# Two-layer decode: last row's kept pairs put between whole pairs, second MLP run for five rows and then three

## Chip, cores, metric

One core of one Trainium2 chip runs one program. The metric is the device time of one launch in microseconds (us). Ratios are the mean time of one kernel's fast runs over that of the other kernel's fast runs of the same rounds, so they are not quite the ratio of the medians quoted beside them. Single executions of the kernel before scattered over 1175.6 to 1181.9 us, so a difference of less than about 2 us needs several rounds, or a comparison inside the traces.

## The reference, cut to what matters

Eight rows (B) of one token each pass twice through attention over a cache and an MLP:

```python
x = x + A(layernorm(x))        # Hq=16, Hkv=8, Sk=4096, Dh=256, D=448
x = x + B(layernorm(x))        # S=1: the shifted part of B is zero, so B is an MLP, 448 -> 1792 -> 448
x = x + A(layernorm(x))        # the same caches again
x = x + B(layernorm(x))

# A, for each row b and each of the 8 cache heads h ("pair" b,h):
#   scores = q @ K[b,h].T / 16 ; p = softmax(scores) ; o = p @ V[b,h]     K, V: 4096 x 256 bf16
# then all heads' o @ wo
```

One pair reads 2 MB of K and 2 MB of V. Almost all of the 472 MB are these.

## The kernel before

All data comes through a ring of five buffers of 1 MB, filled by one DMA queue in a fixed order of chunks. A buffer is refilled when TensorE has used it up. K is transposed on TensorE (`tk`), evicted by VectorE and ScalarE (`ktr`), multiplied with the query (`ps`); then softmax, P*V into `pvb`, and `finish`, which transposes the result into `oT`. For the first 4.5 heads of a row the transposed K stays in SBUF (`keep`), so in the second layer such a *kept pair* needs only V (2 MB, the half-kept one 3 MB), a *whole pair* needs 4 MB. The order of all 128 pairs is fixed when the program is built:

```python
A  = lambda b: [(0, b, h) for h in range(kept_heads, HKV)]     # layer 0, whole
Bk = lambda b: [(0, b, h) for h in range(kept_heads)]          # layer 0, whole, K is kept
C  = lambda b: [(1, b, h) for h in range(kept_heads)]          # layer 1, kept
Dn = lambda b: [(1, b, h) for h in range(kept_heads, HKV)]     # layer 1, whole
...
        for i in range(kept_heads):
            seq += C(b)[i:i + 1]                # kept pairs of row b ...
            if b + 1 < B:
                seq += Bk(b + 1)[i:i + 1]       # ... between whole ones of row b+1
    seq += Dn(B - 1)                            # row 7: five kept pairs in a row, then three whole
```

Row-wise work (layernorm, projections, MLP) is cut into steps. `pump()`, called after each piece of attention, takes one step:

```python
    def outputs(lo, n):                          # o @ wo for n rows: 4 steps of 32 matmuls
        for c in range(KC):
            ...
                for t in range(32):
                    last = e.matmul(room(w, C_Y + c * B + lo, n), wo[:, t, row0(c):row0(c) + w],
                                    copies(oT[:, t // 2, t % 2, lo:lo + n], n), ...)
            op("pe", f, ...)
            yield
    # output(b, h): the same for one pair, 16 matmuls.  mix(lo, n): layernorm and MLP of n rows, 112 matmuls.
    # The matmul counts of outputs and mix do not depend on n.

    def after(g):                                # called when pair g is finished
        layer, b, h = seq[g]
        if layer == 0 or b == B - 1:
            side.append(output(b, h))
        if last_of[layer, b] != g:
            return
        if layer == 0:
            jobs.extend([mix(b, 1), queries(b, 1)])
        elif b == B - 2:
            jobs.extend([outputs(0, B - 1), mix(0, B - 1)])      # rows 0 to 6 at once
        elif b == B - 1:
            jobs.append(mix(B - 1, 1))                           # row 7 at the very end
```

I call `outputs` with the following `mix` *the block* below.

## Time and profile before

| | before |
|---|---|
| median of 3 | 1177.4 us (1176.41 to 1179.94) |
| bytes through the queue | 471.97 MB |
| TensorE (PE) busy | 932 us, 79% |
| last packet of the stream | 1157.9 us (packet records) |
| last P*V | 1159.1 us |
| end | 1175.9 us |

From the page of the kernel before: the span, the busy times, the one data queue, and the shares of the chain that ended last.

```profile
span 1175.9 us, 42204 instructions
...
PE 932.0 (79%) x19067; PEld 811.0 (69%) x19067; DVE 487.6 (41%) x1803; ACT 312.3 (27%) x891; POOL 105.4 (9%) x281
...
q1 hardware_dynamic: 70496, 471.97, 98.0%
...
DMA 51%; PE 35%; DVE 8%; issue 4%; POOL 1%; ACT 0%; SPq 0%; POOLq 0%; ACTq 0%
```

The queue is nearly always full and the chain is half waits for DMA.

The end of the kernel before, in windows of 20 us. The columns are busy time and instruction count of PE (TensorE matmuls), PEld (TensorE weight loads), DVE (VectorE), ACT (ScalarE) and POOL (GpSimd), then the granted TensorE clock, the DMA share, and GB/s.

```profile
1060.00:1080.00 20.00, 17.35 (x361) 15.47 (x365) 11.15 (x49) 6.13 (x17) 1.92 (x5) 1.00 1.02 418
1080.00:1100.00 20.00, 16.97 (x437) 14.14 (x437) 8.38 (x41) 5.17 (x20) 2.87 (x8) 1.00 1.01 415
1100.00:1120.00 20.00, 16.56 (x415) 13.53 (x413) 5.37 (x24) 2.69 (x10) 1.68 (x5) 0.91 0.97 393
1120.00:1140.00 20.00, 16.45 (x308) 14.25 (x305) 9.77 (x44) 4.45 (x13) 2.08 (x5) 0.83 0.89 331
1140.00:1160.00 20.00, 18.30 (x413) 15.61 (x411) 8.45 (x29) 5.79 (x16) 1.54 (x4) 1.00 0.79 303
```

From 1110 on the stream falls from 418 to 331 GB/s: *the hole*. (The 303 of the last window also holds the end of the stream.) The kept pairs of row 7 and the block of seven rows lie there together.

Some TensorE instructions of the same stretch, from the timeline of the kernel before. In brackets stands the idle time before the instruction and what ended it; "issue" means that nothing in the profile was waited for.

```profile
1108.97 0.42 PE L623 MATMUL ps<-qT,keep 128*128 128x48 bf16 x10 [1.87 <-issue]
...
1121.48 0.89 PE L465 MATMUL mm<-oT,wo_sb 128*128 128x21 bf16 x29 [0.87 <-issue]
...
1130.02 0.76 PE L449 MATMUL mm<-oT,wo_sb 128*64 128x24 bf16 x16 [1.89 <-DVE oT L722]
...
1157.91 0.61 PE L697 MATMUL pvb<-ring,pT 128*2 128x256 bf16 x16 [0.36 <-DVE os L718]
...
1159.10 0.61 PE L697 MATMUL pvb<-ring,pT 128*2 128x256 bf16 x16
```

In these lines TensorE stops for 0.9 to 1.9 us three times, inside and around the block. The last two lines are the P*V of the last pair; the last of them begins 16.8 us before the end.

### The profile page before, as it was taken

Reading aid. Unit: us, or ns where it says so; the run is one execution under the profiler, and the core shown is the slowest. Engines: PE = TensorE matmul, PEld = TensorE weight load, DVE = VectorE, ACT = ScalarE, POOL = GpSimd, SP = SyncE. Lnnn points to the kernel's source line nnn. Section 1 sums busy time; section 2 is a strip of 40 time slices with the busy share of each in tenths; the row PEclk is TensorE's granted clock in tenths of the full one; section 3 lists DMA queues with packets and bytes.
Section 4 is the critical chain, followed back from the end, with each engine's and each line's share of the span. In section 5 each row is a group of like instructions: output and inputs, shape, how many; then the busy total and the mean of one; then the engine's idle time right before and its main releaser. Section 6 shows DMA issues by size and latency. Waiting matters only on the chain.

```text
span 1175.9 us, 42204 instructions
## 1 busy us (share of the span) xinstructions
PE 932.0 (79%) x19067; PEld 811.0 (69%) x19067; DVE 487.6 (41%) x1803; ACT 312.3 (27%) x891; POOL 105.4 (9%) x281
## 2 busy tenths in 40 slices
PE   2777898779877887778887887778887887878886
PEld 2666777668766776667776776667766776767675
DVE  2333543345333543345333543345333553345243
ACT  1223322222223222232222322223222222232121
POOL 0000001100100011000110001100110011000100
PEclk8979989999989999999989999999999999999987
DMA  9999999999999999999999999999999999999993
GB/s 359 391 415 419 419 396 417 418 420 412 417 416 420 411 418 410 420 420 404 420 404 420 415 412 416 420 409 412 419 417 420 416 405 417 412 420 414 407 335 133
DMA packets 70676, 474.66 MB, mean 404 GB/s; under 512 B 7248, under 2 KB 13280, under 8 KB 13792
## 3 DMA queue, kind: packets, MB, share of 16 engines
q1 hardware_dynamic: 70496, 471.97, 98.0%
q8 instruction: 149, 2.44, 0.8%
q14 instruction: 31, 0.25, 0.1%
HBM read 471.93 MB, written 0.01 MB: 401 GB/s over the span
## 4 chain that ended last, share of the span: by engine, by line
DMA 51%; PE 35%; DVE 8%; issue 4%; POOL 1%; ACT 0%; SPq 0%; POOLq 0%; ACTq 0%
DMA ring<-in_A_k_cache_dram 51%; PE tk L599 16%; PE ps L623 6%; PE pvb L697 5%; PE mm L449 3%; DVE ktr L606 2%; PE mm L409 2%; PE mm L513 1%; PE pvb L715 1%; DMA ring<-in_A_v_cache_dram 1%; DVE keep L606 1%; DVE oT L722 1%; DVE sm L347 1%; DVE os L718 0%; DVE sm L329 0%
## 5 line engine op out<-in xcount | busy, mean ns | idle before, releaser
L599 PE MATMUL tk<-ident,ring 128*128 128x128 f32 x2944 | 407.5, 291 | 134.0 <-DMA ring<-in_A_k_cache_dram 133.6
L599 PEld LDWEIGHTS tk<-ident,ring 128*128 128x128 f32 x2944 | 343.7, 149 | 177.5 <-DMA ring<-in_A_k_cache_dram 169.3
L606 DVE COPY ktr<-tk 128x512 f32<-128x512 f32 x224 | 153.8, 689 | 192.5 <-PE tk L599 192.4
L604 ACT COPY ktr<-tk 128x512 f32<-128x512 f32 x224 | 129.8, 586 | 323.1 <-PE tk L599 323.0
L697 PE MATMUL pvb<-ring,pT 128*2 128x256 bf16 x4096 | 160.5, 276 | 34.6 <-DMA ring<-in_A_v_cache_dram 22.7
L623 PE MATMUL ps<-qT,keep 128*128 128x48 bf16 x4608 | 159.9, 184 | 5.6 <-issue 4.6
L606 DVE COPY keep<-tk 128x512 f32<-128x512 f32 x144 | 99.5, 691 | 145.3 <-PE tk L599 144.6
L623 PEld LDWEIGHTS ps<-qT,keep 128*128 128x128 bf16 x4608 | 145.3, 97 | 17.6 <-issue 11.5
L604 ACT COPY keep<-tk 128x512 f32<-128x512 f32 x144 | 84.3, 586 | 251.7 <-PE tk L599 251.7
L679 ACT ACTIVATE pT<-ps,nb 128x32 bf16<-128x32 f32 x256 | 76.6, 299 | 268.9 <-DVE nb L675 221.7
L623 PE MATMUL ps<-qT,ktr 128*128 128x48 bf16 x3584 | 129.5, 184 | 17.8 <-DVE ktr L606 8.9
L623 PEld LDWEIGHTS ps<-qT,ktr 128*128 128x128 bf16 x3584 | 115.6, 97 | 29.0 <-DVE ktr L606 22.3
L673 POOL PARTITION_ALL_REDUCE gm<-pm x128 | 45.6, 356 | 796.8 <-DVE pm L670 796.8
L697 PEld LDWEIGHTS pvb<-ring,pT 128*2 128x2 bf16 x4096 | 75.8, 82 | 58.6 <-DMA ring<-in_A_v_cache_dram 27.2
L703 DVE COPY ob<-pvb 128x256 f32<-128x256 f32 x128 | 53.7, 420 | 46.2 <-PE pvb L697 45.6
L684 POOL PARTITION_ALL_REDUCE dn<-rs x128 | 51.2, 400 | 150.8 <-ACT pT L679 150.8
L449 PE MATMUL mm<-oT,wo_sb 128*128 128x24 bf16 (+1 forms) x1152 | 52.7, 187 | 9.5 <-DVE oT L722 4.7
L715 PE MATMUL pvb<-ident,ob 128*128 128x128 f32 x256 | 53.8, 293 | 7.8 <-DVE ob L703 7.5
L409 PE MATMUL mm<-lnT,wq_sb 128*128 128x24 bf16 x864 | 48.2, 184 | 12.9 <-DVE lnT L368 10.2
L670 DVE TENSOR_REDUCE pm<-ps 128x2 f32<-128x64 f32 x128 | 28.6, 224 | 69.1 <-PE ps L623 68.5
L449 PEld LDWEIGHTS mm<-oT,wo_sb 128*128 128x128 bf16 (+1 forms) x1152 | 42.3, 101 | 19.7 <-DVE oT L722 16.6
L409 PEld LDWEIGHTS mm<-lnT,wq_sb 128*128 128x128 bf16 x864 | 39.7, 98 | 22.3 <-DVE lnT L368 10.4
(70 smaller groups left out, 487.3 us busy)
## 6 DMA issues: line engine op xcount, KB each, us to landing
ring<-in_A_v_cache_dram SPq DMA_DIRECT2D x256, 1024.0 KB, 10.3
ring<-in_A_k_cache_dram SPq DMA_DIRECT2D x184, 1024.0 KB, 10.8
wo_sb<-in_A_wo_dram SPq DMA_DIRECT2D x1, 3584.0 KB, 25.6
wq_sb<-in_A_wq_dram SPq DMA_DIRECT2D x3, 1024.0 KB, 11.1
w_sb<-in_B_w_dram SPq DMA_DIRECT2D x1, 1568.0 KB, 20.1
w_sb<-in_B_w_dram SPq DMA_DIRECT2D x3, 448.0 KB, 12.7
wqf_sb<-in_A_wq_dram SPq DMA_DIRECT2D x2, 256.0 KB, 14.3
w3f_sb<-in_B_w_dram SPq DMA_DIRECT2D x2, 112.0 KB, 13.5
```

Source lines behind the costliest of these rows:

```text
L409: last = e.matmul(room(P, at + t * B, n), cols(kc, t), copies(rhs, n), start=(kc == 1), stop=(kc == 0), skip_group_check=True)
L449: last = e.matmul(room(w, C_P + c, 1), wo[:, t, row0(c):row0(c) + w], copies(oT[:, t // 2, t % 2, b:b + 1], 1), start=(t == 4 * h), stop=( ...
L599: last = e.transpose(bank[:, j * P:(j + 1) * P], src[:, 4 * (f % 4) + j, :].bitcast(f32), ident4[:, :])
L604: op("act", lambda e: e.copy(flat, bank[:, :]), reads=[r_bank], writes=[r_kt])
L606: op("dve", lambda e: e.tensor_copy(flat, bank[:, :]), reads=[r_bank], writes=[r_kt])
L623: last = e.matmul(pst[:, at:at + 2 * N_REP].rearrange("p (r j) -> p r j", j=2), kt(i, c), repeated(qT[:, b, c, 2 * h:2 * h + 2]), start=(c ...
L673: op("pool", lambda e: e.partition_all_reduce(gm[q][0][:, :], pm[q][0][:, :], P, ReduceOp.max), reads=[pm[q][1]], writes=[gm[q][1]])
L679: return e.activation(pT[q][0][:, :, :].rearrange("p i j -> p j i")[:, j, :], pst[:, C_S:C_S + 2 * NI].rearrange("p (i j) -> p j i", j=2)[ ...
L684: op("pool", lambda e: e.partition_all_reduce(dn[q][0][:, :], rs[q][0][:, :], P, ReduceOp.add), reads=[rs[q][1]], writes=[dn[q][1]])
L697: last = e.matmul(pvb[at:at + 2, 0:DH], pT[q][0][:, a * HALF + i, :], v[:, i, :], start=(a == 0 and i < 4), stop=(a == 1 and i >= HALF - 4 ...
L703: op("dve", lambda e: e.tensor_copy(ob[:, :], pvb[:, 0:DH]), reads=[r_pv], writes=[r_ob])
L715: last = e.transpose(pvb[:, DH + c * P:DH + (c + 1) * P], ob[:, c * P:(c + 1) * P], ident4[:, :])
```

## The change

The intent: put row 7's kept pairs between whole pairs, as in the other phases, and make a kept pair the last of all, so that no transposes, scores and softmax stand between the last byte and the end. The block moves ahead, to the end of row 4; rows 5, 6 and 7 then send an output by pair and share the last MLP.

```diff
+N_SPARE = 2
+N_ONCE = 5
...
     second = [p_ for b in range(B - 1) for p_ in Dn(b)]
+    second, spare = second[:-N_SPARE], second[-N_SPARE:]
...
+        whole = Bk(b + 1) if b + 1 < B else spare + Dn(b)[:-1]
+        light = C(b)
+        if b == B - 1:
+            light[-2:] = light[:-3:-1]
         for i in range(kept_heads):
-            seq += C(b)[i:i + 1]
-            if b + 1 < B:
-                seq += Bk(b + 1)[i:i + 1]
-    seq += Dn(B - 1)
+            if b == B - 1 and i == kept_heads - 1:
+                seq += Dn(b)[-1:]
+            seq += light[i:i + 1] + whole[i:i + 1]
...
-        if layer == 0 or b == B - 1:
+        if layer == 0 or b >= N_ONCE:
             side.append(output(b, h))
...
-        elif b == B - 2:
-            jobs.extend([outputs(0, B - 1), mix(0, B - 1)])
-        elif b == B - 1:
-            jobs.append(mix(B - 1, 1))
+        elif b == N_ONCE - 1:
+            jobs.extend([outputs(0, N_ONCE), mix(0, N_ONCE)])
+        elif g == len(seq) - 1:
+            jobs.append(mix(N_ONCE, B - N_ONCE))
```

## The prediction

> **What bounds the kernel now.** DMA. The page shows 471.97 MB through one queue, 98% of 16 engines' span, and the chain that ended last is 51% waits for K chunks. Undisturbed 20 us windows move 419 to 422 GB/s. The Trainium skill, "DMA: Bandwidth & Descriptors", section Bandwidth, gives 425 GB/s for a large load with 435 as the fabric ceiling; this trace's plateau agrees. The change leaves the bytes alone; only time in which the queue is not full can be won.
>
> **Where it is not full at the end** (windows view, before): 415 GB/s in 1080-1100, 393 in 1100-1120, 331 in 1120-1140, 303 in 1140-1160 (the stream ends at about 1156.3). Against 419 the stretch 1100-1156.3 misses about 3.05 MB, 7.3 us. Cause, by the timeline: five kept pairs run in a row (ten V chunks issued in a row), then four whole pairs meet the seven-row MLP. PE is busy 9.7, 9.2 and 9.8 us of 10 in 1110-1120, 1130-1140 and 1140-1150, at a granted clock of 0.83 to 0.85 in 1110-1140; it waits 1.9 us for oT behind the layernorm on VectorE, and two "issue" gaps cost 1.3 and 1.9 us. Ring buffers come free 3 to 5 us apart instead of the 2.5 us that a 1 MB chunk takes.
>
> **After the stream:** 1156.3 to 1175.9. The last whole pair has transposes until 1154.8, scores, maximum, exponentials until 1157.6; its P*V runs at 1157.9 and 1159.1, 1.6 and 2.8 us after the last byte. Then 16 us of serial finish, output, layernorm, MLP, store.
>
> **What the change does.**
> - Reorders: kept pairs of row 7 alternate with whole ones (2 and 4 MB), and the last pair is a kept one, needing no K. Its softmax is done before its V lands, so the last P*V should run within 0.3 us of the landing. Gain about 2.5 us.
> - The seven-row output and MLP become five-row ones (4x32 plus 112 matmuls, the same count); the instruction order puts outputs beside pair 6,6 and the MLP beside the next pairs.
> - Adds a 16-matmul output for each pair of rows 5 and 6: 16 x 0.72 us = 11.5 us of PE, 4 us of it in the last 110 us.
> - The end MLP has three rows instead of one: same matmul count and width (copies fill 24 columns), vector work a little wider: +0.1 to 0.4 us.
>
> **On the path.** I expect the queue at 405-415 GB/s in the last 100 us rather than 419: earlier stretches with a one-row MLP show 397 to 406, and PE will be near 90% busy. That gives back about 3 of the 7.3 us: gain 4.5. With the tail 2.5: 7 us. Predicted 1170.5 us, 80% range 1164 to 1176. Chances: faster by over 2% 0.02, within 2% 0.97, slower 0.01.
>
> **What would show it.** Span about 1169. Windows: no 20 us stretch before the stream's end under 385 GB/s; stream over at about 1151-1152; from the last byte to the end about 17 us, not 19.6. The chain's end: DMA of V straight into pvb. PE matmul count +256.
>
> **What would make it wrong.** PE too dense where queries, outputs and MLP fall on alternating pairs, at a lower clock: the hole moves, and the gain is 2 to 3 us. Or the ring, refilled evenly, keeps 419: gain 10 us. Or the "issue" gaps grow. Or a forced wait for the last queries.

## The result

| | before | changed |
|---|---|---|
| median | 1177.49 us, 4 runs | 1177.71 us, 4 runs (1177.27 to 1178.17) |
| ratio | | 0.9999, 95% interval 0.9982 to 1.0016 |
| the same again, five rounds (c_after) | 1177.38 us | 1179.31 us, ratio 1.0018 (1.0006 to 1.0030) |

The predicted 7 us did not appear. The changed kernel is equal or about 0.2% slower, and the measured time lies outside the predicted range.

From the page of the changed kernel: the bytes are the same, and TensorE has 256 matmuls and 20 us of busy time more.

```profile
span 1175.4 us, 42729 instructions
...
PE 951.6 (81%) x19323; PEld 828.7 (70%) x19323; DVE 491.3 (42%) x1819; ACT 312.7 (27%) x891; POOL 105.4 (9%) x281
...
q1 hardware_dynamic: 70496, 471.97, 98.2%
```

The windows of the changed kernel, the same stretches and columns as above.

```profile
1060.00:1080.00 20.00, 17.39 (x378) 14.64 (x377) 10.77 (x50) 5.59 (x18) 2.67 (x7) 1.00 1.01 410
1080.00:1100.00 20.00, 18.36 (x423) 15.62 (x421) 7.52 (x30) 5.04 (x14) 1.51 (x4) 1.00 1.01 415
1100.00:1120.00 20.00, 15.55 (x383) 13.46 (x381) 8.91 (x44) 3.86 (x12) 1.99 (x5) 0.91 0.90 349
1120.00:1140.00 20.00, 19.03 (x421) 16.96 (x416) 8.93 (x28) 5.95 (x17) 1.51 (x4) 1.00 0.99 390
1140.00:1160.00 20.00, 17.24 (x357) 12.98 (x352) 7.25 (x29) 5.04 (x17) 2.27 (x6) 0.88 0.82 340
```

The hole is still there. It came about 20 us earlier, together with the block.

The TensorE timeline of the changed kernel at the same kinds of places.

```profile
1106.09 0.47 PE L631 MATMUL ps<-qT,keep 128*128 128x48 bf16 x12
1108.89 0.67 PE L631 MATMUL ps<-qT,keep 128*128 128x48 bf16 x20 [2.33 <-issue]
...
1118.46 0.72 PE L457 MATMUL mm<-oT,wo_sb 128*64 128x24 bf16 x16 [2.04 <-DVE oT L730]
...
1154.31 0.28 PE L705 MATMUL pvb<-ring,pT 128*2 128x256 bf16 x3 [1.14 <-issue]
...
1156.00 1.02 PE L705 MATMUL pvb<-ring,pT 128*2 128x256 bf16 x16 [0.36 <-DVE os L726]
...
1157.71 1.02 PE L705 MATMUL pvb<-ring,pT 128*2 128x256 bf16 x16
```

Both kinds of gap returned, 2.33 us instead of 1.87 and 2.04 instead of 1.89. The last P*V came 1.4 us earlier than before, but ran for 1.02 us instead of 0.61: TensorE was at half clock.

What that did to the DMA queue, from the timeline of the changed kernel's queue: the times at which a freed buffer was filled again.

```profile
1099.28 0.33 SPq L280 DMA_DIRECT2D ring<-in_A_k_cache_dram  x1
1102.47 0.33 SPq L280 DMA_DIRECT2D ring<-in_A_v_cache_dram  x1
1106.25 0.33 SPq L280 DMA_DIRECT2D ring<-in_A_k_cache_dram  x1
1112.68 1.18 SPq L280 DMA_DIRECT2D ring<-in_A_v_cache_dram  x2
```

At 419 GB/s a chunk of 1 MB takes 2.5 us. Here the refills are 3.2, 3.8 and 6.4 us apart, and the queue runs dry (197 GB/s in 1110-1115).

**A measure for the rest of the text.** The *lag* at time a is when the stream would end if it ran at 419.5 GB/s from a on: a + (471.97 - MB moved until a) / 0.4195. It stands still while the queue is full, and each us by which it grows is a us lost. The MB come from the view of the queues. For the kernel before, from 0 to 1100 and from 0 to 1150 us:

```profile
q1 hardware_dynamic: 67680, 451.62, 100.0%
...
q1 hardware_dynamic: 70127, 469.47, 99.7%
```

At 1100 the lag is 1100 + 20.35 / 0.4195 = 1148.5; at 1150 it is 1156.0. The hole of the kernel before costs 7.5 us, near the prediction's 7.3, which was counted from 1100 to 1156.3. The last column below, the tail, runs from the last data packet (packet records of the trace) to the end of the span. The same for every kernel run:

| run | median us (ratio) | lag growth 60-1060 | 1060-1100 | 1100-1150 | tail |
|---|---|---|---|---|---|
| before | 1177.5 | 16.5 | 0.5 | 7.5 | 18.0 |
| changed, first profile | 1177.7 (0.9999) | 17.3 | 0.9 | 5.1 | 18.2 |
| c_after (changed again) | 1179.3 (1.0018) | 18.3 | 1.9 | 6.7 | 18.2 |
| order_only | 1177.3 (0.9998) | 16.8 | 1.4 | 5.8 | 18.5 |
| split_only | 1180.4 (1.0019) | 23.8 | 0.3 | 2.5 | 17.8 |
| no_mid_mlp | 1174.7 (0.9975) | 17.7 | 0.7 | 0.7 | 18.2 |
| outputs_only | 1178.4 (1.0000) | 19.0 | 1.2 | 4.6 | 18.2 |
| bare_mlp | 1176.1 (0.9989) | 16.7 | 1.6 | 4.8 | 18.2 |
| mlp_only | 1175.6 (0.9978) | 16.7 | 1.0 | 1.3 | 18.2 |
| warm_tail | 1177.6 (0.9996) | 16.6 | 0.7 | 6.6 | 16.8 |
| once4_slow2 | 1179.3 (1.0009) | 21.4 | 1.6 | 0.4 | 18.0 |
| per_pair | 1179.5 (1.0020) | 22.2 | 2.2 | 2.2 | 18.2 |
| fine_outputs | 1179.7 (1.0013) | 16.9 | 1.0 | 5.6 | 19.6 |
| per_pair_warm | 1178.5 (1.0007) | 19.7 | 2.5 | 0.8 | 17.5 |
| before_warm | 1176.3 (0.9989) | 16.1 | 1.1 | 6.2 | 17.9 |
| order_warm | 1176.7 (0.9992) | 16.9 | 0.8 | 5.8 | 16.9 |
| before_no_mid | 1172.3 (0.9955) | 16.5 | 1.1 | 2.4 | 17.7 |

How far to trust it: between 60 and 800 us all kernels but the two per_pair ones run nearly the same pairs and the same work, and in the two profiles of the changed kernel alone the growth from 60 to 1060 was 17.3 and 18.3. I take about 1 us as the scatter of one entry. Two cautions: each row is one profiled execution beside a median of several, and those of mlp_only (1172.9 us) and once4_slow2 (1176.5 us) were the fastest of their runs; and the lag still grows by 1.0 to 3.2 us between 1150 and the last data packet, which the columns leave out.

### The profile page after: what moved, and what is told of

It reads as the page before. It is cut to its first block, busy times and chain, and to the rows that moved or that the text cites. A ratio compares the mean times of both kernels' runs of the same rounds, so it can differ in the third digit from the quotient of the medians.

```text
span 1175.4 us, 42729 instructions
## 1 busy us (share of the span) xinstructions
PE 951.6 (81%) x19323; PEld 828.7 (70%) x19323; DVE 491.3 (42%) x1819; ACT 312.7 (27%) x891; POOL 105.4 (9%) x281
## 3 DMA queue, kind: packets, MB, share of 16 engines
q1 hardware_dynamic: 70496, 471.97, 98.2%
## 4 chain that ended last, share of the span: by engine, by line
DMA 46%; PE 38%; DVE 11%; issue 5%; POOL 1%; ACT 0%; SPq 0%; POOLq 0%; ACTq 0%
DMA ring<-in_A_k_cache_dram 46%; PE tk L607 17%; PE ps L631 7%; PE pvb L705 5%; PE mm L457 3%; DVE ktr L614 3%; PE mm L417 2%; PE mm L521 1%; PE pvb L723 1%; DVE keep L614 1%; DVE oT L730 1%; DVE sm L355 1%; DVE os L726 1%; DVE sm L337 1%; DVE sm L338 1%
## 5 line engine op out<-in xcount | busy, mean ns | idle before, releaser
L607 PE MATMUL tk<-ident,ring 128*128 128x128 f32 x2944 | 415.5, 294 | 118.7 <-DMA ring<-in_A_k_cache_dram 117.5
L607 PEld LDWEIGHTS tk<-ident,ring 128*128 128x128 f32 x2944 | 349.5, 150 | 162.7 <-DMA ring<-in_A_k_cache_dram 152.8
L705 PE MATMUL pvb<-ring,pT 128*2 128x256 bf16 x4096 | 160.6, 277 | 26.7 <-DMA ring<-in_A_v_cache_dram 17.8
L705 PEld LDWEIGHTS pvb<-ring,pT 128*2 128x2 bf16 x4096 | 76.4, 82 | 51.1 <-DMA ring<-in_A_v_cache_dram 22.2
L457 PE MATMUL mm<-oT,wo_sb 128*128 128x24 bf16 (+1 forms) x1408 | 64.4, 187 | 11.7 <-DVE oT L730 5.8
L457 PEld LDWEIGHTS mm<-oT,wo_sb 128*128 128x128 bf16 (+1 forms) x1408 | 51.7, 101 | 24.5 <-DVE oT L730 20.4
```

The costliest lines, as they stand in the source:

```text
L457: last = e.matmul(room(w, C_P + c, 1), wo[:, t, row0(c):row0(c) + w], copies(oT[:, t // 2, t % 2, b:b + 1], 1), start=(t == 4 * h), stop=( ...
L607: last = e.transpose(bank[:, j * P:(j + 1) * P], src[:, 4 * (f % 4) + j, :].bitcast(f32), ident4[:, :])
L705: last = e.matmul(pvb[at:at + 2, 0:DH], pT[q][0][:, a * HALF + i, :], v[:, i, :], start=(a == 0 and i < 4), stop=(a == 1 and i >= HALF - 4 ...
```

## The experiments

### Control and the two halves of the change

**c_after** is the changed kernel, unaltered, with five rounds.

> The changed kernel again, as a control. Its profile lost 1.4 us of stream (0.58 MB) in the first 60 us, where its program does not differ from the kernel before. If that is chance, this second profile should not show it, and the time should still lie within 2 us of the kernel before. If the change gains a little that the first four runs hid, five rounds should show 0.5 to 2.5 us.

Measured: 1179.31 us, 1.0018 (1.0006 to 1.0030). The hole cost 6.7 us. The lag at 60 us was 1132.4, after 1132.8 in the first profile and 1131.5 in the kernel before, so the slow start returned in large part. It is no trait of the changed kernel all the same: order_only, the same program there, had 1131.7, and split_only, which there runs the program of the kernel before, 1132.7. No hidden gain; if anything a loss of 2 us.

**order_only** has the new order and the old split.

```diff
-N_ONCE = 5
+N_ONCE = 7
```

> The new order of pairs, but the MLP for seven rows and then one, as before. Theory 'PE-bound end' (in the last 80 us the TensorE queue, not the DMA, sets the pace, so TensorE work there is what counts): this one has 256 matmuls fewer than the changed kernel but the seven-row MLP later, nearer the end; expected within 2 us of the changed kernel, and a hole of the same 1 to 1.5 MB, now in 1120-1150. Rival 'the order alone helps, the split takes it back': 4 us or more faster than both kernels, about 1172.

Measured: 1177.29 us, 0.9998. The hole moved to 1115-1140 with the block and cost 5.8 us. The order alone gains nothing that can be resolved, so the rival falls. In this trace the deepest stretch follows a TensorE wait of 2.9 us for `ob` on VectorE, which was busy with the layernorm of seven rows; no "issue" gap over 0.8 us lies beside it:

```profile
1122.79 0.69 PE L723 MATMUL pvb<-ident,ob 128*128 128x128 f32 x2 [2.89 <-DVE ob L711]
...
1125.00:1130.00 5.00, 4.73 (x64) 3.98 (x61) 2.71 (x12) 1.17 (x2) 0.00 (x0) 0.67 0.68 234
```

**split_only** has the old order and the new split: the three changed branches of `after` put into the kernel before.

> The old order of pairs, but the MLP for five rows beside the sixth row's phase and three at the end. Theory 'PE-bound end': the MLP work now lies about 40 us earlier than in the changed kernel, amid a stretch with slack, so the hole at the end should shrink, while the tail keeps the softmax chain of the last whole pair: 1173 to 1176. Rival 'the extra outputs of rows 5 and 6 are what the split costs': 1178 or slower.

Measured: 1180.41 us, 1.0019 (1.0006 to 1.0031): slower, which theory did not expect. It is what the rival forecast (1178 or slower), but the trace puts most of the loss at the block's new place and not at the extra outputs. The windows of split_only show it. First the stretch where the block now lies, then the old place of the hole.

```profile
1000.00:1020.00 20.00, 16.96 (x375) 15.01 (x367) 9.82 (x49) 3.85 (x12) 1.98 (x5) 0.86 0.88 319
1020.00:1040.00 20.00, 18.67 (x409) 16.13 (x406) 8.66 (x32) 5.65 (x18) 1.86 (x5) 1.00 0.98 391
...
1100.00:1120.00 20.00, 17.16 (x519) 14.11 (x516) 5.97 (x33) 3.02 (x16) 3.25 (x9) 1.00 0.98 377
1120.00:1140.00 20.00, 16.25 (x355) 14.13 (x355) 7.60 (x27) 5.78 (x18) 2.02 (x6) 1.00 1.01 417
```

The end is nearly whole (417), but 319 GB/s now stand at 1000-1020: the lag grew by 6.4 us between 1000 and 1060. My premise that there was slack for the block 100 us before the end was wrong. The hole goes where the block goes.

### Is the block the hole, or the order?

**no_mid_mlp** is the changed kernel without the block (wrong result: five rows are not finished).

```diff
-            jobs.extend([outputs(0, N_ONCE), mix(0, N_ONCE)])
+            pass
```

> The changed kernel without the outputs and the MLP of the first five rows (wrong result on purpose: five rows stay unfinished). Theory 'PE-bound end': 240 matmuls and the layernorm on VectorE gone from the last 80 us, the hole (300 to 370 GB/s in 1110-1130) closes and the stream ends 3 to 4 us sooner: about 1173.5. Rival 'the hole comes from the alternating order and the two outputs per two pairs': the hole stays and the time stays above 1176.

**before_no_mid** takes the same line out of the kernel before (wrong result).

> The kernel before, old order, without the outputs and the MLP of the first seven rows (wrong result on purpose). Theory 'the block is the hole, the order has no part': the lag grows by 2 us or less in 1100-1150 instead of 7.5, as it did in the changed kernel without its block (0.7 to 1.4), and the time falls by 4 us or more, to 1171-1173.5. Rival, which the prediction rested on, 'five kept pairs in a row start the hole': 3.5 us or more of it stay, time 1174.5 or more.

The windows of no_mid_mlp:

```profile
1100.00:1120.00 20.00, 15.96 (x370) 13.53 (x370) 7.67 (x27) 5.75 (x18) 2.26 (x6) 1.00 1.01 419
1120.00:1140.00 20.00, 15.65 (x295) 13.58 (x292) 8.08 (x22) 6.20 (x16) 1.50 (x4) 1.00 1.01 418
```

The windows of before_no_mid:

```profile
1100.00:1120.00 20.00, 17.34 (x387) 13.33 (x387) 5.06 (x25) 2.49 (x13) 2.27 (x6) 0.78 1.00 387
1120.00:1140.00 20.00, 17.67 (x346) 15.33 (x344) 9.49 (x28) 7.51 (x21) 1.87 (x5) 1.00 1.00 408
```

Without the block, the changed kernel streams at 418 to 419 GB/s (lag growth 0.7, time -4.6 us against c_after). The kernel before, old order and five kept pairs in a row, drops from 7.5 to 2.4 us of lag growth (theory allowed 2, the rival asked for 3.5 or more) and to 1172.3 us (0.9955). So the block is most of the hole in both orders. The old order's own part is at most what stays there, 2.4 - 0.7 = 1.7 us, against 4.5 us that the prediction expected to win by it; and it does not reach the end of the stream: from the lag at 1100 to the last data packet before_no_mid lost 3.5 us (1149.1 to 1152.6) and no_mid_mlp 3.9 us (1150.5 to 1154.4). With the block out of both, the old order is even the faster of the two: 0.9955 (0.9941 to 0.9969) against 0.9975 (0.9962 to 0.9988), in different calls. I have no single cause for that; the changed kernel still has its 256 additional output matmuls there.

### Which part of the block?

**outputs_only** keeps the 128 output matmuls and drops the MLP; **mlp_only** the reverse; **bare_mlp** keeps all matmuls of both and drops the layernorm and GELU on the other engines. Their outputs are wrong, which doesn't matter for the times.

```diff
# outputs_only
-            jobs.extend([outputs(0, N_ONCE), mix(0, N_ONCE)])
+            jobs.append(outputs(0, N_ONCE))
# mlp_only
+            jobs.append(mix(0, N_ONCE))
# bare_mlp: bare_mix = the steps and matmuls of mix, no vector instructions
+            jobs.extend([outputs(0, N_ONCE), bare_mix(0, N_ONCE)])
```

> The changed kernel with the output projection of the first five rows (128 matmuls, 3.7 us) but without their MLP (wrong result on purpose). The lag of the stream (the time it would end at 419 GB/s for the bytes that are left) grew by 5.1 and 6.6 us between 1100 and 1150 in the two profiles of the changed kernel, and by 0.7 with outputs and MLP both gone. Theory 'dense matmuls': the outputs alone give a gap marked issue of over 2 us after them and most of the loss, 2 to 4 us. Rival 'the vector chain of the layernorm': the outputs alone cost under 1 us.

> The changed kernel with all matmuls of outputs and MLP for five rows in the same places, but without the layernorm, the GELU and their waits (wrong result on purpose; the lift matmul goes too). Theory 'dense matmuls' (TensorE work and its issue gap): the lag still grows by 3.5 us or more between 1100 and 1150, the time stays within 1.5 us of the changed kernel. Rival 'the vector chain': the wait of 2.0 us for oT behind the layernorm goes, the lag grows by under 2 us, the time falls by about 3 us.

> The changed kernel with the MLP of five rows, all of its layernorm and matmuls, but without the 128 output matmuls ahead of it (wrong result on purpose). Outputs alone let the lag grow by 4.6 us in 1100-1150, both together by 5.1 to 6.7, neither by 0.7. Theory 'the outputs are most of it, for they come as a burst': 1 to 2.5 us here. Rival 'any 4 us of TensorE work costs about 4 us there, in whichever form': 3.5 us or more.

The windows of outputs_only:

```profile
1100.00:1120.00 20.00, 17.21 (x395) 14.93 (x392) 5.69 (x20) 3.86 (x12) 1.50 (x4) 0.83 0.86 329
1120.00:1140.00 20.00, 17.53 (x357) 15.20 (x354) 8.28 (x23) 6.21 (x16) 1.50 (x4) 1.00 1.01 420
```

The windows of mlp_only:

```profile
1100.00:1120.00 20.00, 16.24 (x367) 13.67 (x365) 10.88 (x52) 5.04 (x18) 2.42 (x7) 0.91 0.99 400
1120.00:1140.00 20.00, 18.43 (x399) 16.35 (x399) 8.49 (x25) 6.10 (x16) 1.84 (x5) 1.00 1.01 417
```

| in the block | lag growth 1100-1150, us |
|---|---|
| nothing | 0.7 |
| MLP alone | 1.3 |
| outputs alone | 4.6 |
| all matmuls, no vector work | 4.8 |
| everything | 5.1, 6.7, 6.6 (three profiles) |

In the changed kernel the output matmuls are most of the hole, not the MLP and not the vector chain. Taking the vector chain away did remove its wait for `oT`; the lag grew by 0.3 to 1.9 us less than with everything. bare_mlp's time, 1176.1, lies 1.6 and 3.2 us under the two medians of the changed kernel, so theory's "within 1.5 us" was missed. They were run at other times. In mlp_only the time fell to 1175.6, 0.9978 (0.9961 to 0.9995). outputs_only's own time, 1178.4, does not resolve its part.

For the old split no run takes the block apart. There the deepest stretch comes later, after the wait for `oT` behind the layernorm (1.89 us, above) and in part at half clock, as in order_only:

```profile
1130.00:1135.00 5.00, 4.98 (x76) 4.29 (x77) 1.99 (x10) 0.69 (x2) 0.00 (x0) 0.66 0.67 226
```

So that the outputs are the larger part there too is not shown. One warning on the side: mlp_only passed the comparison with the reference although five rows lack the attention of the second layer. For these inputs that contribution is below the tolerance, so the comparison would not have found such a mistake.

Why do 128 matmuls that keep TensorE busy for 4.1 us cost 4.6 us? In outputs_only they end in a gap "issue" of 2.6 us (2.33 in the changed kernel), and the clock records show half clock for 6.8 us from 1110.1.

```profile
1111.22 0.98 PE L631 MATMUL ps<-qT,keep 128*128 128x48 bf16 x20 [2.60 <-issue]
```

The Trainium skill, "Runtime: NRT & Kernel Launch", section "Instruction fetch mechanics", says that instructions come in blocks of 16 KiB (256 instructions) over a DMA queue of the sequencer and that the cost is mostly hidden. Here 128 matmuls with their weight loads are just one such block. I compared the 15 gaps of this kind over 0.8 us that I found after 1095 us in nine profiles with the packets of the instruction queue: each gap ended 1.3 to 1.6 us after a 16 KB instruction packet had landed (in the changed kernel: packet 1106.41 to 1107.43, TensorE resumes at 1108.89). The same holds for all 184 gaps of this kind after 60 us in the 17 traces: 1.2 to 1.6 us after such a packet, while the packets come 7 to 8 us apart on average. So TensorE ran out of instructions, as far as a coincidence can show; no run intervened on the fetch alone. Most of these gaps lie beside no burst of outputs.

The half clock after it: the Trainium skill, "TensorE: Matmul & The Clock Gate", Part 1, describes a gate that halves the clock after an idle window of about 3.4 us. The records agree with the window (pieces of 3.4 us). They also show half clock after shorter stops: after the 2.33 us gap the changed kernel had it from 1111.0 to 1114.4, and after the 0.87 us gap at 1120.6 the kernel before had it from 1123.3 to 1126.7, with no other stop in the 3.4 us before.

### Can the work be placed better?

**fine_outputs** splits the 128 output matmuls into 16 steps of 8.

```diff
-        for c in range(KC):
+        for c, k in [(c, k) for c in range(KC) for k in range(4)]:
...
-                for t in range(32):
+                for t in range(8 * k, 8 * k + 8):
```

> A correct kernel: the changed one with the 128 output matmuls in 16 steps of 8 instead of 4 of 32, the same work spread over more than one pair. Theory 'the burst': no gap over 1.2 us marked issue there, the lag grows by 1.5 us or more less than in the changed kernel, 1175 to 1177. Rival 'the work, wherever it lies in the last 60 us': the lag still grows by 5 to 7 us in 1100-1155, time as the changed kernel, 1177 to 1180.

Measured: 1179.72 us, 1.0013 (0.9996 to 1.0030), lag growth 5.6. A gap of 1.69 us stayed (2.33 before), and the MLP slid towards the end. A finer cut in the same stretch does not help: the rival, "the work, wherever it lies in the last 60 us", had forecast this. So it is the output work in this stretch that costs; that its density does is not shown.

**per_pair** lets every pair of the second layer send its own output, so there is no burst at all, for 512 matmuls more.

```diff
-        if layer == 0 or b >= N_ONCE:
-            side.append(output(b, h))
+        side.append(output(b, h))
...
-            jobs.extend([outputs(0, N_ONCE), mix(0, N_ONCE)])
+            jobs.append(mix(0, N_ONCE))
```

> A correct kernel: the changed one, but every pair of the second layer sends its own output of 16 matmuls, so the burst of 128 output matmuls is gone, for 512 matmuls more (about 18 us of TensorE at 36 ns, spread over the whole). Theory 'the burst' (128 matmuls with the scores around them outrun the instruction supply: gap of 2.3 to 2.6 us, then half clock): no issue gap over 1 us in 1100-1115, the lag grows by 3 us or less in 1100-1150 (5.1 and 6.7 in the changed kernel), time 1174 to 1176. Rival 'TensorE work anywhere is the cost': 1180 or slower.

Measured: 1179.54 us, 1.0020 (0.9996 to 1.0044). Both theories were half right. The hole shrank to 2.2 us as expected, but the lag grew by 22.2 us from 60 to 1060 instead of 17 to 18: the additional matmuls took back, a little at a time, what the hole had given.

**once4_slow2** runs the block for four rows, earlier and at half the pace.

```diff
-N_ONCE = 5
+N_ONCE = 4
+    def slow(job, k):
+        for _ in job:
+            for _ in range(k):
+                yield
-            jobs.extend([outputs(0, N_ONCE), mix(0, N_ONCE)])
+            jobs.extend([slow(outputs(0, N_ONCE), 2), slow(mix(0, N_ONCE), 2)])
```

> A correct kernel: the new order, the first MLP for four rows (then four at the end), placed beside the phase of row 6 and taken at half the pace, one step per two turns, so that it spreads over about seven pairs instead of three and a half. Theory 'density': the ring's five buffers (12 us) absorb it, the lag grows by under 3 us there, the end keeps none of the hole: 1174 to 1175.5. Rival 'TensorE has no slack anywhere, the work itself is the cost' (as the run with the old order and the split suggests, which lost 6.4 us in 1000-1060 instead): 1178 to 1180.

Measured: 1179.25 us, 1.0009. The end lost only 0.4 us, but the lag grew by 5.1 us between 900 and 1000, where the kernel before and the changed one lost 2.0 and 2.2. Three placements (here, split_only, the changed kernel), three bills of about 3 to 6 us, after what runs without the block in that stretch lost there is taken off. Within what was tried, TensorE has no slack that takes the block for nothing, although a fifth of the span it is idle.

### The tail

**warm_tail** fills the waits after the stream with 108 matmuls into a bank that nobody reads; **before_warm** does the same to the kernel before.

```diff
+    def warm(k):                       # k matmuls tk[0] <- ident, ident
...
+    warm(12)
     finish(g - 1)
+    warm(8)
     pv(g, 0)
     pv(g, 1)
+    warm(7)
     finish(g)
+    warm(7)
     drain()                            # last mix: warm(60) before its layernorm, warm(14) before its GELU
```

> The changed kernel with 108 idle-filling matmuls (a bank that nobody reads) in the waits after the stream, so that TensorE does not fall to half clock. In both profiles of the changed kernel the half clock begins with the last P*V and lasts to the end. Theory 'half clock eats the tail': the time from the end of the stream to the end falls from 18.2 to about 15.5 to 16 us, 2 us or more of the whole. Rival 'the tail is the vector chain': under 1 us.

> The kernel before with the same 108 idle-filling matmuls in its tail. Its half clock began at 1160.9, after the last P*V. Theory 'the gain of the last pair was real, 0.5 to 1 us, and the half clock, which sets in 5.6 us earlier, took it back': here the tail falls from 18.0 to 17.1-17.4 us, against 16.8 in the changed kernel with the same filling. Rival 'the new last pair gains nothing': 16.8 or less here as well.

The last P*V in warm_tail, and its last MLP matmuls, from the TensorE timeline:

```profile
1158.53 0.61 PE L718 MATMUL pvb<-ring,pT 128*2 128x256 bf16 x16 [1.18 <-DMA ring<-in_A_v_cache_dram]
...
1169.94 1.77 PE L534 MATMUL mm<-hT,w_sb 128*64 128x24 bf16 x56 [0.50 <-DVE hT L525]
```

The last MLP matmuls of the changed kernel, from its own timeline:

```profile
1170.03 2.15 PE L521 MATMUL mm<-hT,w_sb 128*64 128x24 bf16 x56 [1.29 <-DVE hT L512]
```

| us | last packet to last P*V | last P*V to end |
|---|---|---|
| before | 1.2 | 16.8 |
| changed | 0.5 | 17.7 |
| c_after | 0.5 | 17.7 |
| warm_tail | 0.5 | 16.3 |
| before_warm | 1.3 | 16.7 |

The new last pair does what it was meant to do: P*V begins 0.5 us after the last packet instead of 1.2. But with nothing left to transpose or score while it waits for V, TensorE goes idle sooner. The half clock began at 1155.3 instead of 1160.9, and the serial part became 0.9 us longer: 0.7 us from the last P*V to the output matmuls after it, a stretch that now ran at half clock, and 0.2 us in the layernorm, which now has three rows. With the filling the serial part fell by 1.4 us, to 16.3. My expectation for warm_tail (2 us or more) was too high and its rival (under 1 us) too low. before_warm's tail of 17.9 fits neither: its clock fell again at 1168.5, so its filling was worth only about 0.1 us. In times, warm_tail (0.9996) and before_warm (0.9989, 0.9969 to 1.0008) are not resolved from the kernel before.

**per_pair_warm** and **order_warm** combine: outputs by pair, and the new order with the old split, each with the filled tail.

> Outputs by pair and the filled tail together, the version that ought to beat both. If both theories hold the gains add: 1172.5 to 1174.5, 0.3% under the kernel before. If the lag of the stream is bounded by TensorE work elsewhere, it comes out at 1176 or more, with the tail at 16.8 us all the same.

> A correct kernel: the new order, the old split (seven rows and one), and the filled tail. If order and filled tail are each worth what their traces showed, 0.7 and 0.9 us of tail against the kernel before, and the hole costs what it did, then 1175.5 to 1176.5; the kernel before with the filled tail made 1176.3, so a lead over that of under 1 us would not be resolved. If the order helps the stream as well, 1173 or less.

Measured: 1178.54 us (1.0007, 0.9988 to 1.0025) and 1176.74 us (0.9992, 0.9974 to 1.0010). No correct version tried beats the kernel before beyond the noise. The best two, before_warm and order_warm, lie 0.1% under it, inside their intervals.

## Why the prediction was wrong

- **What bounds the kernel: half right.** DMA bytes are the larger share, and the hole's size was right (7.3 predicted from windows, 7.5 by lag). What failed was the sentence "only time in which the queue is not full can be won" taken without its counterpart: the queue is kept full by TensorE, whose busy share of 79% leaves little room. The block costs the stream about 3 to 6 us at each of three places where it was put.
- **"Gain 4.5" from the alternating order: the step that failed.** The hole was put down to five kept pairs in a row, and 397 to 406 GB/s from earlier stretches "with a one-row MLP" were taken for the new rate. Those stretches have no block of 128 output matmuls. The block is most of the hole (7.5 to 2.4 us without it in the old order, 6.7 to 0.7 in the new), and the change kept the block. Three profiles of the changed kernel's stream gave 5.1, 6.7 and 6.6 us, two of the kernel before's 7.5 and 6.2: a mean gain of 0.7 us, within scatter, where 4.5 had been forecast. The prediction's own first line of doubt, "the hole moves", is what happened, and I had given it too little weight.
- **"Gain about 2.5 us" in the tail: mis-sized twice.** The end of the stream was worked out as 1156.3 from GB/s over a window. The packet records have the last data packet at 1157.9, so 1.6 of the 2.8 us that I saw between "last byte" and P*V did not exist. This view of windows in the kernel before shows the remnant that I passed over:

```profile
1157.00:1158.00 1.00, 0.53 (x6) 0.33 (x10) 0.48 (x4) 0.58 (x4) 0.29 (x1) 1.00 0.06 25
```

  The true gain of 0.7 us came; 0.9 was lost behind it (17.7 against 16.8), some 0.7 of it to the half clock, which the prediction did not consider in the tail (16.3 with the clock held up).
- **"Within 0.3 us of the landing": nearly.** It was 0.5 us in each of three profiles.
- **Cost of the additional outputs (11.5 us of PE, off the path):** the count (+256) was right, their busy time 11.7 us (64.4 - 52.7 us in the groups). That they are free was not shown: with the block out, the changed kernel was 2.4 us slower than the kernel before, and 512 more such matmuls went with 3 to 5 us more lag up to 1060 in two profiles (22.2 and 19.7 against about 17).
- **"+0.1 to 0.4 us" for three rows at the end:** consistent; from the last output's addition to the first projection matmul it was 5.0 us before and 5.2 us changed.
- **Chances:** "within 2%" was right, the range of 1164 to 1176 was not.

Left open: whether the instruction fetch makes the gaps "issue" (it was not changed by itself), and how the loss of the output block divides between its 4.1 us of matmuls, the gap and the half clock; also which part of the block makes the hole in the old split.

## What to carry to other kernels

When a stretch of a DMA-bound kernel runs below rate, take out each suspect on its own, in both versions, before reordering: here one deleted line showed that the block, not the order, made the hole. A second engine at 80% can be nearly a second bound: in this kernel, work moved along the stream reappeared as lag wherever it landed, and only taking it out paid. Read the end of a stream from its last packet, not from bytes over rate, and look at the clock in the tail, since work removed there may also let TensorE fall to half clock.

## What the Trainium skill lacked or had wrong

- "Runtime: NRT & Kernel Launch", "Instruction fetch mechanics": block fetches are called mostly hidden. 15 gaps of 0.9 to 2.6 us in nine profiles each ended 1.3 to 1.6 us after a 16 KB instruction packet landed; the packets took about 1.07 us each beside the data stream. The page has no such stop beside a saturated DMA.
- "TensorE: Matmul & The Clock Gate", Part 1: idle of about 3.4 us is given for the drop to half clock. The same Part also tells of short stops between groups of matmuls that make the clock oscillate, without a length. Stops of 0.9 to 2.6 us were followed by 3.4 to 6.8 us of half clock here. For matmuls of 24 columns the half clock cost little (the 48 projection matmuls, from the first start to the last, took 1.28 us at half clock in the changed kernel's tail and 1.19 us at full clock in warm_tail), for P*V with 256 columns much (1.02 against 0.61 us).
- "DMA: Bandwidth & Descriptors", Bandwidth: the 425 GB/s for a large load fits; a stream of 1 MB chunks beside compute held 419 to 422 GB/s, and no page says what part of such a stream a compute block takes away behind five buffers: about 3 to 6 us here, for a block that keeps TensorE busy for 8.5 us (4.1 outputs, 4.5 MLP).
